# Sigmoid attention and a gated FFN on one core: heads as 64 partitions of seven tokens, QK and PV in array quarters, PV first in five bursts a batch

## The chip, the core and the metric

The kernel runs on one core of one Trainium2 chip. The metric is the device time of one execution in microseconds (us). Most executions of one kernel agree within 0.3%. The kernel before took 435.05 us in the median of the three runs (433.63 to 435.94).

## The reference

Eight batches, twelve heads, 448 tokens, head size 64; then an FFN with 768 inputs and 1536 inner units on all 3584 tokens. In float32, cut to its core:

```python
# batch, n_heads, seq, head_dim = 8, 12, 448, 64;  d_model, d_ff = 768, 1536
scores = (1 / sqrt(64)) * q @ k.transpose(0, 1, 3, 2) - log(448)
attn = 1 / (1 + exp(-scores))            # a sigmoid: no sum over the row
x = (attn @ v).transpose(0, 2, 1, 3).reshape(3584, 768)
gate = maximum(x @ w_gate, 0)
out = (gate * (x @ w_val)) @ w_out       # (3584, 768), float32
```

## The kernel before

The work of the kernel is on TensorE, which writes its results into the banks of a memory called PSUM; another engine then "evicts" a bank, that is, reads it out, before it can be filled again. TensorE does QK (scores transposed, keys in partitions), PV, the two products of the gate and the value ("gv", six matmuls of 448 columns each), and the output product ("down"). ScalarE takes the sigmoids and half of the evictions, VectorE the rest. All of it is programmed in one fixed order. From batch 1 on, attention is cut into bursts, and FFN units of earlier batches stand between the bursts, so that ScalarE has time for the sigmoids.

A batch's 448 tokens do not divide by 128. The kernel before puts them in 128 partitions as three and a half blocks: three blocks of 128 keys and a rest of 64 per pair of heads. Two rests of two pairs share one unit ("R"). A unit is two PSUM banks of scores and one sigmoid for each. QK of a block runs in array halves (64 rows by 128 columns), or in quarters (64 by 64) in bursts that also hold PV. PV has its rest blocks in quarters and its full blocks as 128 rows by 64 columns:

```python
def qk_unit(b, unit, quarters):
    ps = [bank("qk_ps") for _ in range(2)]
    ...                                          # the "R" unit: cut
        pr, c = unit
        qkT = qkT_tiles[(b, pr)]
        for hh in range(2):
            rows = slice(64 * hh, 64 * hh + 64)
            step = 64 if quarters else P
            for o in range(0, P, step):
                nc.tensor.matmul(ps[hh][o : o + step, 0:S],
                    qkT[rows, c * P + o : c * P + o + step], qkT[rows, Q0 : Q0 + S],
                    tile_position=(64 * hh, o), ...)
    PT = PTp.tile([P, 2, S], FP16, tag="PT", name="PT")
    for hh in range(2):
        sigmoid(PT[:, hh, :], ps[hh][:, 0:S])

bursts = [((0, 0), (0, 1), ("R", 0)), ((0, 2), (1, 0), (1, 1)), ((1, 2), (2, 0), (2, 1)),
          ((2, 2), (3, 0), ("R", 1)), ((3, 1), (3, 2), (4, 0)), ((4, 1), (4, 2), ("R", 2)),
          ((5, 0), (5, 1), (5, 2))]
pv_at = {0: (-1, 2), 3: (0, 0), 5: (0, 1)}
...
    for m, burst in enumerate(bursts):
        for unit in burst:
            qk_unit(b, unit, m in pv_at)         # three units, six banks
        if m in pv_at and not (m == 0 and b <= 2):
            ...                                  # PV last: the other two banks
        ...                                      # transposes of later pairs by DMA
            ffn_mix(mix[m])
```

The banks come from a pool of eight, handed out in turn; an allocation waits until the last reader of that bank is done. Batch 0 is laid out differently: 112 partitions of four tokens, two halves of 224 queries, transposed on TensorE. Batch 1 is transposed on TensorE too, and from batch 2 on VectorE copies keys and queries together ("rel") and a DMA transposes them ("qkT").

## Time and profile before

| | before |
|---|---|
| time, median of 3 runs | 435.05 us |
| span of the profiled execution | 432.6 us |
| TensorE busy | 423.6 us, 98% |
| DMA-transposed pairs (36), median from issue to landing | 4.0 us |
| first sigmoid starts at | 7.22 us |

The span can be cut where the gv work on batch 1 and on batch 2 begins, since both kernels pass these points with nearly the same work done (the changed kernel is four QK units, 0.76 us, ahead at the first point and one, 0.19 us, at the second). This is the view of three stretches of the kernel before. Its columns are the stretch, its length, the busy time and number of instructions of TensorE, of its weight loads, of VectorE, ScalarE and GpSimd, then the granted clock, the DMA share and GB/s.

```profile
0.00:67.53 67.53, 63.39 (x744) 45.99 (x744) 31.57 (x91) 47.62 (x88) 37.92 (x60) 1.00 1.32 184
67.53:118.32 50.79, 50.23 (x339) 24.78 (x337) 19.90 (x55) 27.79 (x62) 20.27 (x34) 1.00 1.01 134
118.32:432.60 314.28, 309.99 (x1994) 160.16 (x1992) 100.06 (x241) 138.96 (x304) 44.94 (x72) 1.00 0.50 78
```

The reader is to see the full clock in all three stretches, and a TensorE that is idle for some 4 us in each of the first and the last stretch.

### The profile page before, as it was taken

The numbers are of one execution on the slowest core, as the hardware profiler recorded it, in microseconds if no ns is written. First come the engines' busy times: TensorE is split into PE (matmuls) and PEld (weight loads), VectorE is DVE, ScalarE is ACT, GpSimd is POOL, SyncE is SP. The second block draws the span as 40 slices with busy tenths as digits, with TensorE's granted clock in tenths as the row PEclk, the third lists the DMA queues.
The fourth block names the chain that finished last, engine by engine and source line by source line (L and its number), as shares of the span: only waits on it lengthen the run. The fifth ranks groups of instructions, "written<-read, shape, count | busy, mean of one in ns | idle before, by whom it ended". The sixth has DMA issues, their size and how long they took to land.

```text
span 432.6 us, 7728 instructions
## 1 busy us (share of the span) xinstructions
PE 423.6 (98%) x3071; PEld 230.9 (53%) x3071; DVE 151.5 (35%) x385; ACT 214.4 (50%) x452; POOL 103.1 (24%) x165
## 2 busy tenths in 40 slices
PE   8899999999999999999999999999999999999996
PEld 3579765454555455455455555455454554555563
DVE  2473644334242333334242332433233322222111
ACT  5774783566544554645454453654635446122110
POOL 8454816273070201720053200710000000000000
PEclk9999999999999999999999999999999999999999
DMA  9999999699298821996169550992212411100134
GB/s 185 197 196 196 131 202 167 80 146 234 65 145 106 123 59 40 158 116 97 21 95 179 87 91 17 135 131 66 58 44 49 83 23 36 38 0 2 49 98 109
DMA packets 91940, 43.83 MB, mean 101 GB/s; under 512 B 58432, under 2 KB 88320, under 8 KB 91904
## 3 DMA queue, kind: packets, MB, share of 16 engines
q0 software_dynamic: 52896, 23.14, 44.0%
q1 hardware_dynamic: 38448, 19.67, 23.8%
q10 hardware_dynamic: 560, 0.52, 0.4%
q8 instruction: 24, 0.39, 0.4%
q14 instruction: 12, 0.10, 0.1%
HBM read 47.19 MB, written 11.01 MB: 135 GB/s over the span
## 4 chain that ended last, share of the span: by engine, by line
PE 91%; DMA 4%; ACT 2%; DVE 1%; issue 0%; ACTq 0%
PE g_ps L358 26%; PE v_ps L358 24%; PE ya L412 16%; PE yb L412 8%; PE qk_ps L306 6%; PE pv_ps L341 6%; DMA qkT<-rel 4%; ACT PT L191 2%; PE qk_ps L220 1%; PE pv_ps L327 1%; PE pv_ps L238 1%; PE warm_ps L174 1%; PE qk_ps L290 1%; DVE qkT L207 1%; PE trt L277 1%; DVE xT L182 0%
## 5 line engine op out<-in xcount | busy, mean ns | idle before, releaser
L191 ACT ACTIVATE PT<-qk_ps 128x448 f16<-128x448 f32 (+1 forms) x318 | 154.0, 589 | 26.1 <-PE qk_ps L306 21.4
L358 PE MATMUL g_ps<-xT,wg 128*128 128x448 f16 (+1 forms) x648 | 127.7, 333 | 0.2 <-DVE xT L182 0.2
L358 PE MATMUL v_ps<-xT,wv 128*128 128x448 f16 (+1 forms) x648 | 126.8, 332 | 0.0
L376 DVE TENSOR_TENSOR hT<-gate_sb,v_ps 128x448 f16<-128x448 f32 (+1 forms) x108 | 61.2, 569 | 161.4 <-PE v_ps L358 91.7
L367 ACT ACTIVATE gate_sb<-g_ps 128x448 f32<-128x448 f32 (+1 forms) x102 | 53.4, 531 | 78.9 <-PE g_ps L358 78.7
L412 PEld LDWEIGHTS <-hT 128*128 128x128 f16 x672 | 65.7, 98 | 47.2 <-issue 0.4
L358 PEld LDWEIGHTS <-wg 128*128 128x128 f16 x648 | 58.5, 98 | 57.2 <-issue 19.1
L358 PEld LDWEIGHTS <-wv 128*128 128x128 f16 x648 | 63.2, 98 | 46.4 <-issue 0.4
L412 PE MATMUL ya<-wo,hT 128*128 128x512 f16 x336 | 77.1, 379 | 0.0
L426 ACT ACTIVATE ysb<-yb 128x256 f32<-128x256 f32 x28 | 10.7, 384 | 105.2 <-PE yb L412 105.2
L182 DVE TENSOR_SCALAR xT<-pv_ps 128x448 f16<-128x448 f32 (+1 forms) x54 | 29.7, 573 | 46.5 <-PE pv_ps L341 41.1
L412 PE MATMUL yb<-wo,hT 128*128 128x256 f16 x336 | 41.3, 273 | 0.0
L420 DVE TENSOR_SCALAR ysb<-ya 128x512 f32<-128x512 f32 x28 | 19.4, 692 | 56.7 <-PE ya L412 56.7
L306 PE MATMUL qk_ps<-qkT 64*64 64x448 f16 (+1 forms) x336 | 33.0, 357 | 0.1
L112 POOL DMA_DIRECT2D v<-in_v_dram x13 | 9.1, 699 | 94.6 <-PE pv_ps L341 66.4
L341 PE MATMUL pv_ps<-PT,v 128*64 128x448 f16 x252 | 27.8, 357 | 0.0
L106 POOL DMA_DIRECT2D k<-in_k_dram x15 | 10.3, 686 | 35.4 <-DVE rel L260 32.2
L341 PEld LDWEIGHTS <-v 128*64 128x64 f16 x252 | 12.5, 109 | 11.3 <-issue 5.0
L306 PEld LDWEIGHTS <-qkT 64*64 64x64 f16 (+1 forms) x336 | 9.1, 99 | 16.5 <-issue 13.3
L119 POOL DMA_DIRECT2D v<-in_v_dram x21 | 13.3, 635 | 16.9 <-DMA q<-in_q_dram 12.0
L118 POOL DMA_DIRECT2D v<-in_v_dram x21 | 13.5, 641 | 8.9 <-DMA wo<-in_moe_w_out_dram 6.4
L117 POOL DMA_DIRECT2D v<-in_v_dram x21 | 14.0, 665 | 0.0
(44 smaller groups left out, 171.4 us busy)
## 6 DMA issues: line engine op xcount, KB each, us to landing
out_dram<-ysb SPq DMA_DIRECT2D x48, 192.0 KB, 2.7
wg<-in_moe_w_gate_dram POOLq DMA_DIRECT2D x6, 384.0 KB, 10.2
wv<-in_moe_w_val_dram POOLq DMA_DIRECT2D x6, 384.0 KB, 10.6
wo<-in_moe_w_out_dram POOLq DMA_DIRECT2D x1, 1536.0 KB, 11.9
k<-in_k_dram POOLq DMA_DIRECT2D x6, 256.0 KB, 5.2
q<-in_q_dram POOLq DMA_DIRECT2D x6, 256.0 KB, 6.9
v<-in_v_dram POOLq DMA_DIRECT2D x21, 64.0 KB, 7.4
k<-in_k_dram POOLq DMA_DIRECT2D x9, 128.0 KB, 5.5
```

Source lines behind the costliest of these rows:

```text
L117: nc.gpsimd.dma_start(v16[64:P, odd, :], hi[:, o, :])
L118: nc.gpsimd.dma_start(v16[64:P, even, 0:KLO], hi[:, e, 0:KLO])
L119: nc.gpsimd.dma_start(v16[0:64, even, KLO:], hi[:, e, KLO:])
L182: nc.vector.tensor_scalar(out=xT_of(b, pr)[:, q0 : q0 + qn], in0=src, scalar1=XSCALE, scalar2=None, op0=AOP.mult,)
L191: nc.scalar.activation(PT_ap, ps_ap, AF.Sigmoid, bias=sig_bias, scale=qk_scale)
L306: nc.tensor.matmul(ps[hh][o : o + step, 0:S], qkT[rows, c * P + o : c * P + o + step], qkT[rows, Q0 : Q0 + S], start=True, stop=True, tile ...
L341: nc.tensor.matmul(ps[r][64 * hh : 64 * hh + 64, 0:S], v16[:, 2 * pr + hh, c * D : (c + 1) * D], PT[:, hh, :], start=False, stop=(c == 2), ...
L358: nc.tensor.matmul(ps[-1][:, 0:qn], wt[:, dc, f * P : (f + 1) * P], xT_tiles[(b, dc)][:, q0 : q0 + qn], start=(dc == 0), stop=(dc == NDC - 1),
L367: nc.scalar.activation(gate_sb[:, 0:qn], ps[0][:, 0:qn], AF.Relu)
L376: nc.vector.tensor_tensor(out=hT_tiles[(g, f)][:, o : o + qn], in0=gate_sb[:, 0:qn], in1=ps[1][:, 0:qn], op=AOP.mult,)
L412: nc.tensor.matmul(ps[:, 0 : m1 - m0], hT_tiles[(g, f)][:, t * P : (t + 1) * P], wo[:, f, m0:m1], start=(f == 0), stop=(f == NFC - 1),)
L420: nc.vector.tensor_scalar(out=ysb[:, m0:m1], in0=ps[:], scalar1=OUT_SCALE, scalar2=None, op0=AOP.mult)
```

## The change

Every batch is laid out as 64 partitions of seven tokens per head, with two pairs of heads side by side in 128 partitions (a "group" of four heads; three groups a batch). All of QK and PV can then run in array quarters. The intent is plain from the kernel before: one tiling mode for a whole burst, five bursts instead of seven, hence fewer changes of mode, and no rest blocks. PV stands first in its burst. Batch 0 is cut into 192 and 256 queries, and has six slots of four units instead of twelve of two. The core of the diff, cut at "...":

```diff
-    CH = 112
-    NCH = S // CH
+    NCH = S // 64
+    QCUT = 3
+    HALVES = ((0, QCUT), (QCUT, NCH))
...
+    def load(b, g0, g1, which="kqv", c0=0):
+        for nm, t16, src in zip("kqv", tiles_of(b), (k, q, v)):
+            if nm in which:
+                for g in range(g0, g1):
+                    for r in range(2):
+                        nc.gpsimd.dma_start(
+                            t16[64 * r : 64 * r + 64, g, :, c0 * D :],
+                            rows_of(src, b, r)[:, g, :, c0 * D :],
+                        )
...
+    def qk(qkT, r, hh, c, c0, c1, out_ap):
+        rows = slice(64 * hh, 64 * hh + 64)
+        cols = slice(64 * r, 64 * r + 64)
+        nc.tensor.matmul(out_ap, qkT[rows, c, cols], qkT[rows, NCH + c0 : NCH + c1, cols],
+            tile_position=(64 * hh, 64 * r), ...)
+
+    def pv(b, g, q0, qn, pieces):
+        ps = [bank("pv_ps") for _ in range(2)]
+        for c in range(NCH):
+            for hh in range(2):
+                for r in range(2):
+                    rows = slice(64 * r, 64 * r + 64)
+                    nc.tensor.matmul(ps[r][64 * hh : 64 * hh + 64, 0:qn],
+                        v16[rows, g, hh, c * D : (c + 1) * D], pieces[c][rows, hh, :],
+                        start=(c == 0), stop=(c == NCH - 1),
+                        tile_position=(64 * r, 64 * hh), ...)
+        for r in range(2):
+            put_xT(b, 2 * g + r, q0, qn, ps[r][:, 0:qn])
...
+        cuts = (0, 4, 7, 11, 16, 21) if b <= 2 else (0, 4, 8, 12, 16, 21)
+        pv_at = {0: -1, 3: 0, 4: 1} if b <= 2 else {0: -1, 2: 0, 4: 1}
...
+        for m in range(5):
+            if m in pv_at and (b, m) != (1, 0):
+                ...                              # PV first
+            for g, c in order[cuts[m] : cuts[m + 1]]:
+                qk_unit(b, g, c)                 # four or five units
+            if b == 1:
+                if m == 0:
+                    load(2, 0, 1, "kq")
+                    load_o()                     # the output weights, 2.3 MB
+                    load(2, 1, 2, "kq")
+                    ...
+                if m == 3:
+                    dma_transposes(2, 0)
```

Batch 2 begins with the PV of batch 1 and QK of its own first group. Its first group is transposed by a DMA during batch 1.

## The prediction

> **What bounds the kernel now.** I read the page first: its list of engines, then the chain of work that ended last, then the waits of TensorE.
>
> ```profile
> PE 423.6 (98%) x3071; PEld 230.9 (53%) x3071; DVE 151.5 (35%) x385; ACT 214.4 (50%) x452; POOL 103.1 (24%) x165
> ...
> PE 91%; DMA 4%; ACT 2%; DVE 1%; issue 0%; ACTq 0%
> ```
>
> ```profile
> PE qk_ps L220 <- DVE qkT L207: 1.8, 3, 0.7
> PE warm_ps L174 <- DVE zeros L137: 1.2, 1, 1.2
> PE qk_ps L220 <- ACT PT L191: 0.4, 1, 0.4
> PE qk_ps L290 <- DMA qkT<-rel: 0.4, 1, 0.4
> PE g_ps L358 <- DVE xT L182: 0.2, 1, 0.2
> ```
>
> The reader is to see that TensorE carries 91% of the chain, and that its listed waits add up to 4.0 us of 432.6. From batch 2 on it waits for nobody. So what counts is matmul time, what stands between matmuls, and any new wait. The next view is the timeline of TensorE in a steady stretch (start, length, engine, line, op; an entry's length includes the matmul's pipeline tail, so I take differences of starts):
>
> ```profile
> 194.67 0.35 PE L358 MATMUL v_ps<-xT,wv 128*128 128x448 f16 x1
> 194.95 0.74 PE L306 MATMUL qk_ps<-qkT 64*128 64x448 f16 x6
> 195.63 1.31 PE L358 MATMUL g_ps<-xT,wg 128*128 128x448 f16 x6
> 196.77 1.30 PE L358 MATMUL v_ps<-xT,wv 128*128 128x448 f16 x6
> ...
> 200.50 1.47 PE L412 MATMUL yb<-wo,hT 128*128 128x256 f16 x12
> 201.90 0.57 PE L306 MATMUL qk_ps<-qkT 64*64 64x448 f16 x8
> 202.31 0.36 PE L290 MATMUL qk_ps<-qkT 64*64 64x448 f16 x4
> 202.49 0.36 PE L327 MATMUL pv_ps<-PT,v 64*64 64x448 f16 x4
> 202.78 1.33 PE L341 MATMUL pv_ps<-PT,v 128*64 128x448 f16 x12
> 204.04 1.31 PE L358 MATMUL g_ps<-xT,wg 128*128 128x448 f16 x6
> ```
>
> Six full matmuls of 448 columns take 1.14 us, 0.19 each. Four quarters together also take 0.19 (202.31 to 202.49), and so does a pair of halves. I call 0.19 a slot. A burst without PV runs from 194.67 to 195.63, 0.96 us, in which are the last full matmul and three slots, 0.76: 0.20 are lost at its two borders. A burst with PV starts when the last of twelve yb matmuls of 0.109 does, at 201.70, and ends at 204.04: 2.34 less 0.11 and ten slots of 0.19 leaves 0.33, for three borders (202.49 to 202.78 is 0.29 where 0.19 would do). With the slightly longer first full matmuls after it I count 0.21 and 0.35.
>
> **What the Trainium skill says.** "TensorEngine Tiling (Array Packing)", Key Properties: changing the tiling mode, not just the tile, drains TensorE. The trace agrees: about 0.1 us per border, and none between QK and PV quarters. "TensorE: Matmul & The Clock Gate", Back-to-back issue gap: N/2.4 + 2.5 ns, 189 ns for 448 columns; the trace has 190. Same page, Part 3, What overlaps and what doesn't: matmuls keep strict order, so one that waits holds all behind it; the waits above do not contradict it. "PSUM — Partial Sum Buffer", Specifications: 8 banks per partition, a matmul output at most one. No run shows the number 8, but the program names eight banks, and the kernel before fits them exactly: three QK units of two banks plus PV's two.
>
> **The change part by part.**
>
> *Matmul work, batches 1 to 7: nothing.* 147 QK units and 21 PV groups of 7 slots stay 147 slots each. TensorE gets 3660 matmuls instead of 3071, since quarters go four to a slot; that costs nothing here, as four quarters took the 0.19 of two halves.
>
> *Borders: a saving.* Before: 49 bursts, 19 of them with PV, and two PV groups alone: 30 x 0.21 + 21 x 0.35 = 13.7 us. After: 35 bursts and one PV alone, all in quarters: 36 x 0.21 = 7.6. Saved **6.1 us**. The transposes of batch 1 become column halves with their own borders, 3 x 0.2 = 0.6 back.
>
> *PSUM banks: a new wait.* A burst now has four or five QK units, so 8 or 10 banks, and with PV 10 or 12. In order: PV takes two, units 0, 1 and 2 the other six, and unit 3 needs a bank that PV just filled. I let the changed kernel's instructions be listed with their banks and waits: of 20 PV bursts, unit 3 gets both PV banks in 10; in the other 10 it gets one PV bank and the first bank of unit 0, and the second PV bank goes to what comes next. When are they free? These are the timelines of VectorE and ScalarE:
>
> ```profile
> 195.13 0.62 DVE L376 TENSOR_TENSOR hT<-gate_sb,v_ps 128x448 f16<-128x448 f32 x1 [1.65 <-PE v_ps L358]
> ...
> 203.58 1.19 DVE L182 TENSOR_SCALAR xT<-pv_ps 128x448 f16<-128x448 f32 x2 [2.19 <-PE pv_ps L341]
> ```
>
> ```profile
> 195.35 2.73 ACT L191 ACTIVATE PT<-qk_ps 128x448 f16<-128x448 f32 x6 [0.88 <-PE qk_ps L306]
> ```
>
> The first pair's last PV slot starts at 202.78 + 0.21 + 0.19 = 203.18, its eviction 0.40 later; two evictions take 1.19. In the new PV both banks fill in the same last slot; call its start s. The evictions end at s + 1.02 and s + 1.59, and a semaphore adds some 0.04. TensorE would reach unit 3 at s + 4 x 0.19 = s + 0.76. Where it needs both banks it loses 1.63 - 0.76 = 0.87 us. In the other case: unit 0 starts at s + 0.19, its sigmoid 0.40 later, and lasts about 0.54 (six take 2.73, overlapped), so unit 3 goes at s + 1.17, a loss of 0.41, and the unit or FFN matmul after it loses 0.15 to 0.25 on the second PV bank: 0.6. Sum: 10 x 0.87 + 10 x 0.6 = **14.7 us**.
>
> *The same in bursts without PV.* Of these, 13 have a fourth unit that takes the bank of the FFN unit just before. Its eviction starts 0.46 after the last matmul (194.67 to 195.13) and takes 0.62, free at 1.12; TensorE arrives at 0.28 + 0.20 + 0.19 + 0.19 = 0.86. 13 x 0.26 = **3.4 us**.
>
> Both lie wholly on TensorE, which has no slack to absorb them.
>
> *Batch 0: about even.* Here ScalarE sets the pace: 24 sigmoids of 2 x 448 at 0.85 us, 20.4 us. From 0.455 for 448 columns and 0.85 for 896 I estimate 0.88 ns a column plus 0.06: 0.74 for 768, 0.96 for 1024. The new three slots of 192 and three of 256 queries then take 3 x (3 x 0.74 + 0.40) + 3 x (3 x 0.96 + 0.51) = 18.0. TensorE saves 1.1 us: 96 slots of 0.096 become 42 of 0.083 or 0.109. Against it: between the units now stand about a dozen pieces of 0.6 to 1.2 us (14 transpose pairs, a PV, an FFN unit), two score buffers let TensorE run only two units ahead, and only 4 FFN units of 192 queries fill this stage instead of 6 of 224. I estimate 0.2 to 0.5 us of ScalarE waiting at most of them, about what is gained: 0, give or take 2. Some 1 us of ScalarE-made gaps in batch 1 (53.04 to 54.16 in the timeline) may go too.
>
> *Transfers: hidden.* Input pieces grow from 384 or 512 bytes to 896 in the tile, which can only help; the relay copies halve in number; the tail is unchanged.
>
> Sum: -6.1 + 0.6 + 14.7 + 3.4 + 0 - 1 = +11.6 us on 435.05.
>
> **The rivals.** *First, the borders win:* bank waits are small because PV goes first and three units cover its eviction. Then only -6.1 + 0.6 - 1 counts, 428 to 430. Against it: three slots are 0.57 us, and two evictions plus their start 1.59. For it: whoever ordered PV first meant this. *Second, batch 0 decides:* queries of 192 let FFN start after three slots instead of six; a stage without ScalarE gaps would give 2 to 3 us, one with more of them, or inputs landing late behind more than a dozen small loads of 0.7 us issue each, would cost as much. *Third, quarters cost more than a slot* because QK's queries are now read in runs of 64 instead of one run of 448: 0.02 us on 147 slots would be 3 us more. The old bursts have four quarters in 0.19, but never such reads. *Fourth, a transfer blocks VectorE:* the copies for batch 2 stand in batch 1's fourth burst, about when its keys land behind the weights (estimate from 193 KB per us: near 50 us); a delay of 3 us there would still hide behind free banks.
>
> **Range and chances.** The mechanism is firm, its size rests on four measured durations and a count of bursts. If the bank waits are a third smaller, +5.6; if batch 0 also loses 2 us and quarters cost more, +16. I predict **446 us**, range 437 to 454. Slower by 2% means over 443.8: chance 0.64. Within 2%: 0.30. Faster by 2% (under 426.3) would need no waits and a better batch 0: 0.06.
>
> **What would show it.** In the new profile TensorE's waits must list QK behind VectorE's eviction of PV, about 20 times, up to 0.9 us, together with about 13 behind the FFN's product and 10 behind sigmoids, 15 to 20 us in all; border gaps must still be 0.1, five pairs a batch; four quarters must start 0.19 apart. Batches 2 to 7 should take some 10 us longer together. If there are no such waits, or if the time before batch 1's first QK changes by more than 3 us, I was wrong in that step.

## More of the kernel before

Some executions differ by the clock granted to TensorE (1.00 is full), of which the text tells where it matters.

Batch 2 begins with the PV of batch 1 and five FFN units ahead of its first QK.

## The result, and the profile after

The changed kernel took **451.80 us** in the median of four runs (449.25 to 454.94), beside 434.76 us (433.63 to 435.94, four runs) for the kernel before. The ratio is 1.0395, with a 95% interval of 1.031 to 1.048: slower. A ratio here is the mean time of one kernel's runs over that of the other's in the same rounds, so it is not quite the ratio of the medians that I quote. The four executions fall into two kinds: two with a mean granted clock of 0.98 took 453.81 and 454.94, two with 0.999 took 449.25 and 449.79. The profiled one is of the slower kind.

From the page of the changed kernel: engines, clock in 40 slices, and the chain of work that ended last.

```profile
PE 434.1 (96%) x3660; PEld 241.8 (53%) x3660; DVE 129.6 (29%) x247; ACT 211.9 (47%) x453; POOL 97.7 (22%) x163
...
PEclk8599998999999999999999999999999999999999
...
PE 87%; DMA 5%; DVE 3%; ACT 3%; issue 1%; ACTq 0%
```

Against the page of before, TensorE gave up four points of the chain, and VectorE, ScalarE and DMA took them. The clock row has two dents: slices 1 and 2, and slice 7. The kernel before had none. The waits of TensorE after:

```profile
PE qk_ps L215 <- DVE xT L167: 4.8, 29, 0.2
PE qk_ps L215 <- DMA qkT<-rel: 2.4, 1, 2.4
PE trt L190 <- ACT k L380: 2.4, 1, 2.4
...
PE trt L190 <- DVE q L381: 0.9, 1, 0.9
```

The first line is the predicted wait, QK behind the eviction of PV. The second is a wait on the DMA transposes of batch 2's first group, and the third and fourth are waits for the first keys and queries. The stretches after, cut at the same points:

```profile
0.00:76.54 76.54, 66.99 (x989) 48.41 (x989) 27.49 (x67) 46.44 (x92) 41.01 (x68) 0.91 1.23 176
76.54:129.10 52.56, 51.62 (x388) 26.35 (x385) 15.23 (x30) 26.43 (x60) 21.97 (x38) 0.97 1.03 138
129.10:453.10 324.00, 315.46 (x2291) 167.03 (x2288) 86.88 (x152) 139.02 (x305) 34.72 (x59) 1.00 0.40 71
```

So the profiled execution lost 9.0 us up to the FFN of batch 1, 1.8 us in the second stretch and 9.7 us in the last, which runs at full clock. The last stretch is what I had predicted to lose. The first one I had called about even.

**The bank waits.** Here is a burst with PV, and one without, in TensorE's timeline of the changed kernel:

```profile
92.74 1.23 PE L215 MATMUL qk_ps<-qkT 64*64 64x448 f16 x16
93.91 1.31 PE L293 MATMUL g_ps<-xT,wg 128*128 128x448 f16 x6
...
102.45 1.52 PE L232 MATMUL pv_ps<-PT,v 64*64 64x448 f16 x28
103.80 0.74 PE L215 MATMUL qk_ps<-qkT 64*64 64x448 f16 x12
104.69 0.35 PE L215 MATMUL qk_ps<-qkT 64*64 64x448 f16 x1 [0.15 <-DVE xT L167]
105.22 0.57 PE L215 MATMUL qk_ps<-qkT 64*64 64x448 f16 x7 [0.18 <-DVE xT L167]
```

And VectorE's timeline at that time:

```profile
104.01 1.16 DVE L167 TENSOR_SCALAR xT<-pv_ps 128x448 f16<-128x448 f32 x2 [2.07 <-PE pv_ps L232]
```

PV's last slot begins at 103.80 less 0.19, that is 103.61; three units of four quarters follow at 103.80; the fourth would start at 103.80 + 3 x 0.19 = 104.37. It has its first matmul at 104.69 and its second at 105.22, when the second of VectorE's two evictions is done (104.01 + 1.16 = 105.17). The delay is 0.85 us, though the wait that the view prints is only 0.15 + 0.18. The printed idle begins where the previous matmul's modelled end lies, 0.35 us after its start, so short waits look far smaller than they are. Only differences of starts tell the loss. This is why the sum of 4.8 us in the list of waits explains only part of the 9.7 us.

I therefore computed for each burst from batch 3 on: the start of the first FFN matmul behind it, less the start of the last one before it, less 0.19 for each slot of four quarters or two halves and the time of that last FFN matmul. This is the mean loss per burst in us (with its count; a burst is named by its number of QK units):

| | before | after |
|---|---|---|
| QK alone, three units | 0.20 (20) | |
| QK alone, four units | | 0.50 (10) |
| three units and PV | 0.36 (14) | |
| four units and PV | | 0.78 (5), 1.10 (5) |
| five units and PV | | 1.06 (5) |

**The transfer.** The same timeline where batch 2 begins:

```profile
71.26 1.52 PE L232 MATMUL pv_ps<-PT,v 64*64 64x448 f16 x28
75.20 1.40 PE L215 MATMUL qk_ps<-qkT 64*64 64x448 f16 x16 [2.42 <-DMA qkT<-rel]
76.53 2.24 PE L293 MATMUL g_ps<-xT,wg 128*128 128x448 f16 x6
78.57 2.09 PE L293 MATMUL v_ps<-xT,wv 128*128 128x448 f16 x6
80.50 1.30 PE L293 MATMUL g_ps<-xT,wg 128*128 128x448 f16 x6
```

The DMA transposes were issued at 59.71 and TensorE got their result at 75.20. Besides the wait itself, six matmuls of 448 columns now take 2.04 us (76.53 to 78.57) instead of 1.14: TensorE was put to half clock, and stayed there until about 80.2.

### The profile page after: what moved, and what is told of

The parts are those of the page before. It is cut to its first block, busy times and chain, and to the rows that moved or that the text cites.

```text
span 453.1 us, 8742 instructions
## 1 busy us (share of the span) xinstructions
PE 434.1 (96%) x3660; PEld 241.8 (53%) x3660; DVE 129.6 (29%) x247; ACT 211.9 (47%) x453; POOL 97.7 (22%) x163
## 3 DMA queue, kind: packets, MB, share of 16 engines
q0 software_dynamic: 32960, 23.28, 36.8%
## 4 chain that ended last, share of the span: by engine, by line
PE 87%; DMA 5%; DVE 3%; ACT 3%; issue 1%; ACTq 0%
PE g_ps L293 24%; PE v_ps L293 23%; PE ya L331 16%; PE yb L331 8%; PE qk_ps L215 7%; PE pv_ps L232 7%; DMA qkT<-rel 3%; DVE xT L167 3%; ACT PT L176 3%; PE trt L190 2%; DMA ysb<-in_q_dram 1%; DVE qkT L195 0%; ACTq L110 0%; PE warm_ps L159 0%; ACT ysb L345 0%
## 5 line engine op out<-in xcount | busy, mean ns | idle before, releaser
L176 ACT ACTIVATE PT<-qk_ps 128x448 f16<-128x448 f32 (+3 forms) x318 | 150.8, 596 | 65.2 <-PE qk_ps L215 65.1
L293 PE MATMUL g_ps<-xT,wg 128*128 128x448 f16 (+2 forms) x648 | 128.5, 334 | 0.8 <-DVE xT L167 0.2
L293 PE MATMUL v_ps<-xT,wv 128*128 128x448 f16 (+2 forms) x648 | 127.6, 333 | 0.0
L311 DVE TENSOR_TENSOR hT<-gate_sb,v_ps 128x448 f16<-128x448 f32 (+2 forms) x108 | 60.9, 569 | 229.0 <-PE v_ps L293 118.5
L302 ACT ACTIVATE gate_sb<-g_ps 128x448 f32<-128x448 f32 (+2 forms) x104 | 55.3, 549 | 73.1 <-PE g_ps L293 71.3
L215 PE MATMUL qk_ps<-qkT 64*64 64x448 f16 (+2 forms) x756 | 56.2, 347 | 9.1 <-DVE xT L167 4.8
L215 PEld LDWEIGHTS <-qkT 64*64 64x64 f16 x756 | 25.3, 110 | 38.2 <-issue 25.9
L232 PE MATMUL pv_ps<-PT,v 64*64 64x448 f16 (+2 forms) x756 | 38.1, 338 | 0.1
L167 DVE TENSOR_SCALAR xT<-pv_ps 128x448 f16<-128x448 f32 (+2 forms) x54 | 28.4, 568 | 23.2 <-PE pv_ps L232 23.2
L97 POOL DMA_DIRECT2D q<-in_q_dram x48 | 28.8, 622 | 18.7 <-DMA wo<-in_moe_w_out_dram 15.8
```

The source lines that it names most:

```text
L97: nc.gpsimd.dma_start(t16[64 * r : 64 * r + 64, g, :, c0 * D :], rows_of(src, b, r)[:, g, :, c0 * D :],)
L167: nc.vector.tensor_scalar(out=xT_of(b, pr)[:, q0 : q0 + qn], in0=src, scalar1=XSCALE, scalar2=None, op0=AOP.mult,)
L176: nc.scalar.activation(PT_ap, ps_ap, AF.Sigmoid, bias=sig_bias, scale=qk_scale)
L215: nc.tensor.matmul(out_ap, qkT[rows, c, cols], qkT[rows, NCH + c0 : NCH + c1, cols], start=True, stop=True, tile_position=(64 * hh, 64 * r ...
L232: nc.tensor.matmul(ps[r][64 * hh : 64 * hh + 64, 0:qn], v16[rows, g, hh, c * D : (c + 1) * D], pieces[c][rows, hh, :], start=(c == 0), sto ...
L293: nc.tensor.matmul(ps[-1][:, 0:qn], wt[:, dc, f * P : (f + 1) * P], xT_tiles[(b, dc)][:, q0 : q0 + qn], start=(dc == 0), stop=(dc == NDC - 1),
```

## The experiments

Twelve kernels ran, all with correct results. My theory at first was that banks explain the last stretch, and that batch 0 with its late first loads explains the first one. The rivals were that the order PV first is harmless and something else in the quarters costs the time, and that the first stretch is lost to the transfer. Each result below stands beside 433.6 to 434.5 us for the kernel before in the same rounds.

**Seven bursts of three units, PV still first.** No burst needs more than eight banks then.

```diff
-        cuts = (0, 4, 7, 11, 16, 21) if b <= 2 else (0, 4, 8, 12, 16, 21)
-        pv_at = {0: -1, 3: 0, 4: 1} if b <= 2 else {0: -1, 2: 0, 4: 1}
+        cuts = (0, 3, 6, 9, 12, 15, 18, 21)
+        pv_at = {0: -1, 3: 0, 5: 1}         # and the FFN units shared out over seven
```

> The changed kernel with seven bursts of three QK units a batch instead of five of four or five; PV still first and all in quarters, so PV and three units fill exactly eight banks. Bank theory: the waits for PV's eviction (0.6 to 0.9 us in each of 20 bursts) and for the FFN product go, some 15 to 17 us, and 14 more bursts cost 14 x 0.21 = 2.9 us: 436 to 440 us against 451.8. Rival (quarters, strided query reads or batch 0 cost the time, not banks): 452 to 456 us.

Measured: 442.38 us (439.27 to 445.85), ratio 1.0192 (1.0124 to 1.0259). The waits of TensorE in this run:

```profile
PE qk_ps L215 <- DMA qkT<-rel: 3.4, 1, 3.4
PE g_ps L293 <- DVE xT L167: 3.1, 20, 0.2
```

QK no longer waits for the eviction of PV. But now the FFN product behind each of the 20 PV bursts gets PV's bank, and waits in its place: such a burst loses 0.44 us, where borders alone cost 0.22. The bank theory holds in kind; the time came out 2.4 us above my range because I had not asked who gets the bank next, and because the wait on the transfer grew from 2.4 to 3.4 us. The clock plays a part too: the two executions at 0.994 and 0.997 took 439.27 and 440.57 us, the two at 0.979 took 444.19 and 445.85.

**PV two units behind in its burst, nothing else.**

```diff
-            if m in pv_at and (b, m) != (1, 0):
-                ...                              # PV
-            for g, c in order[cuts[m] : cuts[m + 1]]:
+            ahead = 2
+            for n, (g, c) in enumerate(order[cuts[m] : cuts[m + 1]]):
+                if n == ahead and m in pv_at and (b, m) != (1, 0):
+                    ...                          # PV
                 qk_unit(b, g, c)
```

> The changed kernel with the same instructions and the same five bursts, only PV moved behind two QK units of its burst instead of before them all. Bank theory: PV's banks are then asked for again only in the fifth unit or the FFN after the burst, where they come from a unit whose sigmoids are done, so the PV waits shrink from about 0.7 to under 0.2 us a burst: 437 to 441 us. The waits of 0.26 us in bursts without PV stay. Rival (the burst's length or the quarters as such cost the time): 450 to 453 us, as no instruction is added or taken away.

Measured: 442.57 us (440.85 to 443.92), ratio 1.0192 (1.0158 to 1.0225). A burst of five units and PV in its timeline:

```profile
110.82 0.57 PE L215 MATMUL qk_ps<-qkT 64*64 64x448 f16 x8
111.22 1.49 PE L232 MATMUL pv_ps<-PT,v 64*64 64x448 f16 x28
112.54 0.98 PE L215 MATMUL qk_ps<-qkT 64*64 64x448 f16 x12
113.46 1.31 PE L293 MATMUL g_ps<-xT,wg 128*128 128x448 f16 x6
```

No wait of QK on an eviction of PV is left in the list. Four units with PV lose 0.22 us now, which is the two borders, and five lose 0.47. From batch 2's FFN to the end the profiled run took 314.8 us, against 324.0 with PV first and 314.3 before. So 9.2 of the 9.7 us of the last stretch are the order of PV and the banks. The quarters themselves cost no more than a slot: eight of the new kind, with their queries in runs of 64, take 0.40 us (110.82 to 111.22), two slots of 0.19 and 0.02.

**PV three units behind (a dose).**

```diff
-            ahead = 2
+            ahead = 3
```

> A dose test of the bank theory: the changed kernel with PV behind three QK units of its burst instead of two. Bank theory: with two units ahead TensorE waited for no PV eviction (442.6 us). With three ahead, PV takes the banks of the last FFN product, whose eviction is not over, so each of the 20 PV bursts waits about 0.26 us again, as the bursts without PV do: 447 to 448 us with a wait of PV on the FFN product in the list, and no QK wait on the eviction of PV. Rival (what counts is only that PV is not first in its burst): the same as with two ahead, 442 to 443 us.

Measured: 447.86 us (444.10 to 449.27), ratio 1.0308 (1.0252 to 1.0364). The same place in its timeline:

```profile
109.81 0.76 PE L215 MATMUL qk_ps<-qkT 64*64 64x448 f16 x12
110.40 1.77 PE L232 MATMUL pv_ps<-PT,v 64*64 64x448 f16 x28
111.83 0.72 PE L215 MATMUL qk_ps<-qkT 64*64 64x448 f16 x8
```

PV's 28 matmuls stretch from 1.32 to 1.43 us by their starts. The starts of single matmuls in this trace show why: the first one is at 110.40, the second, which writes the other bank, only at 110.66. VectorE's eviction of the FFN product (hT) had ended at 110.60. By my sum over starts, a burst of four units with PV loses 0.50 us instead of 0.22 and one of five 0.59 instead of 0.47. The list of waits does not print this wait, since the first matmul's modelled end covers it, so that part of the expectation missed. That the time was right is luck in part: two of the four runs had clocks of 0.974 and 0.977, and the two at 0.99 took 444.10 and 446.57 us. In the stretch from batch 2's FFN to the end, 318.7 us against 314.8 and both at full clock, the dose costs 3.9 us. It is the bank that counts, not the mere place of PV.

**The first loads.** The second group's loads, which share the DMA engines with the first group's, are held until the first keys are there.

```diff
-    load(0, 1, 2, "kq")
     ident = const.tile([P, P], FP16, name="ident")
     make_identity(nc, ident[:])
+    hold = const.tile([P, 2], FP32, name="hold")
+    nc.gpsimd.tensor_copy(hold[0:1, :], k32[1][0:1, 0:2])
+    load(0, 1, 2, "kq")
```

> The changed kernel with GpSimd's loads of the second group held back until the first key rows have landed. Theory: the first head group landed late (8.5 us against 6.4) because these loads now start 2 us earlier on the same engines and share them; then the first sigmoid moves from 10.55 to 7.5 to 8.5 us and the time falls by 2 to 3.5 us, 448 to 450 us. Rival (loads of 64 partitions land late by themselves): first sigmoid stays at 10 us or later, time 451 to 454.

Measured: 451.41 us (450.86 to 454.31), ratio 1.0411 (1.0372 to 1.0451): no gain. The first sigmoid did start at 7.44 instead of 10.55 us. Its waits:

```profile
PE trt L192 <- DMA q<-in_q_dram: 2.7, 2, 1.5
PE qk_ps L217 <- DMA qkT<-rel: 1.9, 1, 1.9
```

The second group is late in its turn, and the first FFN unit started only 1.1 us earlier (23.28 for 24.34). That the loads as a whole pace the early stage would fit this, but is not shown: the granted clock differs too, half from 12.7 to 16.1 and from 19.5 to 22.9 us here, from 8.5 to 22.1 us in the changed kernel. Behind the wait of 1.9 us the clock stayed full.

**Batch 2's first group transposed on TensorE instead of by DMA.**

```diff
-                if m == 3:
-                    dma_transposes(2, 0)
+            hooks = {..., 4: [(1, lambda: both(2, 0))]}    # 28 transposes on TensorE
```

> The changed kernel with the first group of batch 2 transposed on TensorE (two times 28 quarter-width transposes, about 1.1 us) instead of by a DMA that landed 15 us after its issue. Theory: the gap of 2.4 us before batch 2's first QK goes, and with it the half clock after it (1.7 us in the profiled run): 447 to 450 us and a mean granted clock of 0.99 or more. Rival (the gap moves to the next transfer, group 1 of batch 2): TensorE waits for qkT at the next burst by about as much, time 450 to 453.

Measured: 450.30 us (448.98 to 452.32), ratio 1.0362 (1.0332 to 1.0392). The wait on the transfer and the second dent in the clock are gone, and the profiled run reached batch 1's FFN at 75.02 instead of 76.54 us, batch 2's FFN at 125.58 instead of 129.10. The second number is the one to read, since the half clock came behind the first point. Both profiled runs had half clock at the start, and the whole span fell by 3.0 us (450.1 for 453.1), as much as the wait and the half clock less the transposes seemed to be worth (2.4 + 1.7 - 1.0). The medians fell by 1.5 us only. Two executions of each kernel had a clock of 0.999, and there the transposes on TensorE gained nothing: 450.09 and 450.51 us against 449.25 and 449.79. No such execution was profiled.

**Bursts of five and three.** PV two behind, the transposes on TensorE, and from batch 3 on no burst without PV that has a fourth unit.

```diff
-        cuts = ... else (0, 4, 8, 12, 16, 21)
+        cuts = ... else (0, 5, 8, 13, 16, 21)
```

> PV two units behind, batch 2's first group transposed on TensorE, and from batch 3 on bursts of 5, 3, 5, 3 and 5 units, so that no burst without PV has a fourth unit. Bank theory: 442.6 less 1.5 (the transposes, as measured alone) less 10 x 0.27 (the fourth units) = 438 to 439 us; from batch 2's FFN to the end about 312 us against 314.8 with two ahead alone and 314.3 before. Rival (fourth units lose nothing that counts; fifth units lose more): 441 us, about 315 us.

Measured: 435.70 us (435.44 to 437.64), ratio 1.0051 (1.0020 to 1.0082). This is 3 us better than I expected, but not for my reason. The last stretch took 314.0 us, not 312: QK alone lost 0.22 us per burst as hoped, but every PV burst now had five units and lost 0.47. The gain was up to batch 1's FFN (72.15 for 75.40 us with PV two behind alone). With PV two behind, the transfer's wait had been 4.4 us; taking it away was worth more than in the run before, where it had been 2.4.

**Batch 0 as the kernel before has it**, whole, with its 112 partitions, its loads and its schedule; once on top of the last kernel, and once as the only thing undone.

```diff
-        self.g, (self.c0, self.c1) = g, HALVES[half]     # 64 x 7 tokens, 192 and 256 queries
+        self.pr, self.q0 = pr, q0                        # 112 x 4 tokens, 224 and 224 queries
...                                                       # with load_first, first_transposes, the loop
```

> The kernel of the run above, with batch 0 as the kernel before has it whole: 112 partitions of four tokens, halves of 224 queries, its loads, its schedule; batches 1 to 7 in quarters. Theory (what is left of the loss lies in the new batch 0 and its loads): first sigmoid near 7.2 us, the first FFN of batch 1 near 69 instead of 75 us, 431 to 433 us in all, below the kernel before. Rival (the loss before batch 1's FFN comes from the quarter layout of batch 1, or from the weights and inputs landing as before): 436 us or more.

Measured: 434.61 us (434.30 to 435.83), ratio 1.0021 (0.9995 to 1.0048): as fast as the kernel before, no faster, and 1.1 us faster than with the new batch 0, less than the 3 to 5 us that I had expected. The first FFN of batch 1 came at 69.35 us as expected; the remaining 1.8 us against the kernel before are four QK units of batch 2 moved forward, 0.76 us, and 1.0 us of transposes that a DMA did in the kernel before.

> The changed kernel with nothing undone but batch 0, which is as the kernel before has it whole. Theory (batch 0 carries 5 to 7 of the 17 us): 444 to 447 us, the first FFN of batch 1 near 70 us instead of 76.5, and from batch 2's FFN to the end still about 324 us. Rival (batch 0 is even, as I predicted): 450 to 452 us.

Measured: 451.52 us (449.53 to 452.32), ratio 1.0392 (1.0353 to 1.0432): no gain over the changed kernel in the medians. My theory of the first stretch, which asked for 444 to 447 us, fell here. This is its timeline:

```profile
66.60 1.52 PE L244 MATMUL pv_ps<-PT,v 64*64 64x448 f16 x28
71.77 1.71 PE L227 MATMUL qk_ps<-qkT 64*64 64x448 f16 x16 [3.65 <-DMA qkT<-rel]
73.41 2.42 PE L337 MATMUL g_ps<-xT,wg 128*128 128x448 f16 x6
```

With the old batch 0, TensorE comes to this point 4.7 us earlier (PV at 66.60 for 71.26), and waits 3.65 us for the transfer instead of 2.42, again with half clock behind it. The transposes were issued 3.3 us earlier (56.43 for 59.71) and again took 15 us. So 1.2 of the 4.7 us were spent on waiting, and the whole span of this profiled execution is 3.1 us shorter (450.0 for 453.1). The medians are even because two executions of the changed kernel, at a clock of 0.999, took 449.25 and 449.79 us, no more than the one at 0.998 here (449.53). They were not profiled; that the late transfer hides the slow start there would fit, but is not shown.

**The transfer held apart from the weights.** The same kernel, and GpSimd issues the output weights and the rest of batch 2 only when the transposes have landed.

```diff
                 if m == 3:
                     dma_transposes(2, 0)
+                    nc.gpsimd.tensor_copy(gate[0:1, :], qkT_tiles[(2, 0)][0:1, 0, 0:2])
+                    load(2, 1, 2, "kq")
+                    load_o()
+                    ...                          # the rest of batch 2, moved here from m == 0
```

> The changed kernel with batch 0 as before (451.5 us when run alone), and one thing more: GpSimd starts the loads of the output weights and of the rest of batch 2 only when the DMA transposes of batch 2's first group have landed. Transfer theory (the transposes were not hidden because they shared the DMA engines with 2.3 MB of output weights issued just before them): they land 5 to 7 us after their issue instead of 17, TensorE's wait of 3.7 us on them and the stretch of half clock after it go, the first FFN of batch 1 starts near 68.5 instead of 73.4 us, and the time is 446 to 447 us. Rival (the transposes are slow in themselves, or the wait is paid later when the held loads land late): 450 to 452 us.

Measured: 450.49 us (450.34 to 451.49, five runs), ratio 1.0377 (1.0360 to 1.0393). The time is the rival's; the mechanism is the theory's. These two lines of its profile are the issue of the transposes, on SyncE, and the first instruction of GpSimd that waits for them:

```profile
56.48 15.87 SPq L220 DMA_TRANSPOSE qkT<-rel  x2
61.00 0.17 POOL L504 COPY gate<-qkT 1x2 f16<-1x2 f16 x1 [11.97 <-DMA qkT<-rel]
```

They took 4.5 us (56.48 to 61.00) instead of 15.3 (56.43 to 71.77 in the run before). So the loads issued ahead of them were what made them late; the weights and the other loads of batch 2 were held together, and which of the two counts is not set apart. The first group was in time, with no wait, and batch 1's FFN started at 69.73 instead of 73.41 us. Then the held loads came late. TensorE and VectorE of this run, 15 us on:

```profile
84.25 0.56 PE L227 MATMUL qk_ps<-qkT 64*64 64x448 f16 x5
87.27 1.65 PE L227 MATMUL qk_ps<-qkT 64*64 64x448 f16 x11 [2.46 <-DVE hT L355]
```

```profile
76.82 0.62 DVE L355 TENSOR_TENSOR hT<-gate_sb,v_ps 128x448 f16<-128x448 f32 x1 [1.65 <-PE v_ps L337]
85.23 0.39 DVE L216 COPY rel<-k 128x896 f16<-128x896 f16 x1 [7.79 <-DMA k<-in_k_dram]
```

VectorE stood for 7.79 us before the copy of keys that had not landed. The FFN products behind it in its queue stayed in their banks, and QK waited for those banks. Most of the gain was lost again 15 us later, by another way (batch 2's FFN began at 124.62 instead of 125.89 us): a late transfer blocked VectorE, which was my fourth rival, only not where I had put it.

**The transposes on TensorE, with the old batch 0.** This takes the transfer away without making another one late.

```diff
+        # batch 0 as before, whole
-                if m == 3:
-                    dma_transposes(2, 0)
+            hooks = {..., 4: [(1, lambda: both(2, 0))]}
```

> The changed kernel with batch 0 as before and with batch 2's first group transposed on TensorE, its loads as in the changed kernel: nothing is held, so nothing lands later. In the run with batch 0 alone the wait on the DMA transposes was 3.7 us and the half clock after it cost about 1.7; the transposes on TensorE cost about 1.0. Theory (the transfer's wait and its half clock are real time): 451.5 - 5.4 + 1.0 = 447 us, the first FFN of batch 1 near 70 us; what is left against the kernel before, some 12.5 us, is then the bank waits less the borders. Rival (the wait only moves again): 450 to 451 us.

Measured: 446.72 us (446.39 to 447.25, five runs, all with a clock of 1.000), ratio 1.0291 (1.0271 to 1.0310), as the theory had it to 0.3 us. Its stretches:

```profile
0.00:70.20 70.20, 65.08 (x889) 48.20 (x890) 28.79 (x72) 48.05 (x91) 39.66 (x64) 1.00 1.29 191
70.20:121.06 50.86, 49.92 (x384) 25.85 (x384) 15.74 (x31) 26.31 (x59) 19.26 (x34) 1.00 1.02 137
121.06:444.70 323.64, 315.45 (x2291) 167.12 (x2288) 86.89 (x152) 139.02 (x305) 34.71 (x59) 1.00 0.41 71
```

The clock is full throughout. Of the 12.1 us that this profile is longer than that of the kernel before, 9.4 are in the last stretch and 2.7 in the first, of which 1.8 are the four QK units and the transposes named above. So taking the transfer away gained 451.5 - 446.7 = 4.8 us with the old batch 0. The transposes on TensorE took some 1.0 us of that back, so I estimate the late transfer itself at 5.8 us, and what remains of 446.7 - 434.1 = 12.6 us for the bursts at 11.6.

**A version that uses what was learned.** From batch 2 on six bursts of 4, 3, 4, 3, 4, 3 units, PV two behind in those of four, the transposes on TensorE; once with the old and once with the new batch 0.

```diff
+        cuts = (0, 4, 7, 11, 16, 21) if b == 1 else (0, 4, 7, 11, 14, 18, 21)
+        pv_at = {3: 0, 4: 1} if b == 1 else {0: -1, 2: 0, 4: 1}
```

> Batch 0 as before, batches from 2 on in six bursts of 4, 3, 4, 3, 4, 3 units, PV two units behind in those of four. From the losses measured per burst (0.22 us for three units alone and for four with PV two behind, 0.50 for four alone, 0.47 for five with PV): a batch loses 6 x 0.23 = 1.4 us instead of 1.9, so about 2.7 us less than the 434.6 of the same kernel in bursts of five and three: 431.5 to 432.5 us, 0.4 to 0.6% below the kernel before. Rival (each burst's borders cost the same whatever its units): 435 us or more.

Measured: **431.28 us** (431.04 to 432.46, six runs), ratio 0.9931 (0.9917 to 0.9945): 0.7% faster than the kernel before, with an interval clear of 1. A burst with PV, and the last stretch:

```profile
131.51 0.57 PE L227 MATMUL qk_ps<-qkT 64*64 64x448 f16 x8
131.92 1.49 PE L244 MATMUL pv_ps<-PT,v 64*64 64x448 f16 x28
133.24 0.55 PE L227 MATMUL qk_ps<-qkT 64*64 64x448 f16 x8
133.72 1.31 PE L337 MATMUL g_ps<-xT,wg 128*128 128x448 f16 x6
```

```profile
117.63:428.90 311.27, 307.17 (x2292) 162.12 (x2288) 88.12 (x155) 138.62 (x304) 35.94 (x60) 1.00 0.41 74
```

From batch 2 on every burst with QK loses 0.22 us now, with PV or without, and the last stretch is 3.0 us shorter than before. This is what the quarters save here.

> The same six bursts with the new batch 0 (the changed kernel's layout throughout, batch 2's first group transposed on TensorE). Theory: 2.7 us less than the 435.7 of the same kernel in bursts of five and three, 432.5 to 434 us; and 0 to 2 us slower than the run with batch 0 as before, which is then what the new batch 0 costs. Rival (batch 0 costs 5 us or more): 437 us or more.

Measured: 433.65 us (432.09 to 434.58, six runs), ratio 0.9978 (0.9957 to 0.9999). It falls into two kinds again: 432.09, 432.42 and 432.91 us at clocks of 0.998 and 0.999, and 434.39, 434.50 and 434.58 at 0.982 and 0.983. The profiled execution is of the second kind:

```profile
8.00:12.00 4.00, 3.73 (x52) 2.15 (x52) 1.18 (x5) 1.62 (x2) 4.00 (x7) 0.50 1.21 188
12.00:16.00 4.00, 3.58 (x64) 2.26 (x56) 1.43 (x3) 2.78 (x4) 4.00 (x7) 0.50 1.27 174
```

With the old batch 0 no execution is of this kind (0.998 to 1.000 in all six). So the new batch 0 costs about 1.1 us at full clock (mean 432.5 less 431.4) and 3.1 us when half clock is granted in the start, which happened in three of six executions.

## Why the prediction was right or wrong

The prediction named the class (slower, 0.64) and its range held the time; 446.0 stands against 451.8. The mechanism that it named is there, at the size that it named. That the range held although a whole term was missing is owed to the range's width. By its own steps:

- *PSUM banks, +14.7, and bursts without PV, +3.4:* right. Against 0.22 us of borders, a PV burst lost 0.56 or 0.88 us more (I had 0.6 and 0.87), one of five units 0.84, and four units alone 0.28 (I had 0.26). Giving each kind its third of 20 PV bursts, that is 20/15 x (5 x 0.56 + 5 x 0.88 + 5 x 0.84) = 15.2 us, and 13 x 0.28 = 3.6. Taking only PV's place back removed 9.2 of the 9.7 us in the last stretch, and the dose run put 3.9 of them back. The list of waits shows 29 waits on the eviction of PV, but none on the FFN product, for which the prediction had asked about 13 times; they are there in the starts of single matmuls (in the burst at 92.74, the fourth unit's second matmul starts at 93.59 instead of 93.33, behind an eviction that ended at 93.54).
- *Borders, -6.1:* right in size. They cost 0.22 us per burst in quarters, where I had 0.21; the six-burst version shows them as a gain when no wait covers it.
- *The sum of these steps* was +11.6 us. The run that has only them, with the old batch 0 and no transfer to wait for, shows +12.6 (446.72 against 434.09), or 11.6 without its 1.0 us of transposes: it is the kernel that I had in fact predicted. So close a match is luck in part, since the terms as measured, -6.1 + 0.6 + 15.2 + 3.6, add up to 13.3.
- *"Transfers: hidden"* is the step that failed. I had looked at sizes of pieces and number of copies, and not at when batch 2's first keys are needed. In the kernel before, the PV of batch 1 and five FFN units stand ahead of batch 2's first QK; in the new one nothing does, and the DMA transposes share their engines with 2.3 MB of output weights. The term is some +5.8 us instead of 0 (estimate above): a wait of 2.4 us in the changed kernel and 3.7 with the old batch 0, and half clock behind it for 3.4 and 5.6 us. With the loads held back, the same transposes landed after 4.5 us instead of 15.3.
- *"Batch 0: about even", 0 give or take 2:* the medians are even, 451.80 against 451.52 with the old batch 0, but the profiled executions are not, 453.1 against 450.0. In the six-burst kernel it costs 1.1 us at full clock and 3.1 with half clock in the start. I had counted sigmoids (18.0 instead of 20.4 us), and neither the first loads nor the clock.
- *I had said that a change of more than 3 us before batch 1's first QK would mean that I was wrong in that step.* This sign did not show: the first QK came at 38.44 instead of 37.61 us. It was badly chosen, since the changed kernel had by then done only 6.5 us of FFN products instead of 10.3 (in slots of 0.19). The delay came to light later: PV at 71.26 instead of 66.60 us with the old batch 0, and +9.0 us up to batch 1's FFN against the kernel before, the wait on the transfer included.
- *"From batch 2 on it waits for nobody"* misread the kernel before a little: two of its PV bursts lost more than the usual 0.33 us, 1.08 at 103.76 and 0.58 at 187.72.
- *ScalarE's gaps in batch 1, -1:* not settled. No run sets it apart.

In the medians, the old batch 0 alone gained 0.3 us, the transposes on TensorE alone 1.5, and both together 5.1 (446.72); in the profiled executions it is 3.1, 3.0 and 8.4 us. Two delays of which one hides the other would do this, but no execution of the changed kernel with a clock of 0.999 was profiled, so what those wait for stays open.

## What to carry to other kernels

Before putting more work between two stretches of other work, count the PSUM banks in order of allocation, and ask for each bank who read it last and who gets it next; moving one product two units back in its burst was worth 9 us here, the same product three units back lost 4 of them again. When a change pulls the first use of a tile forward, look up when its transfer lands, not how long it takes, and expect that removing one delay uncovers another behind it. A list of waits understates short waits: measure bursts by the starts of matmuls.

## What the Trainium skill lacked or had wrong

- "TensorEngine Tiling (Array Packing)", Key Properties, says that changing the tiling mode drains TensorE, but not what it costs: 0.20 us for a burst of halves with its two borders, 0.22 us for one of quarters, and 0.34 us with three borders, the same to 0.01 us in nearly all of the 34 bursts with QK that were measured in the kernel before.
- "TensorE: Matmul & The Clock Gate", What's actually happening, has half clock come after an idle window of about 3.4 us. Here gaps of 2.4 us (changed kernel, at 75.20) and 2.5 us (loads held, at 87.27) were enough, while one of 1.9 us (first loads, at 73.81) was not. The half clock after the first lasted from 76.8 to 80.2 us, 3.4 us, which agrees with that page's window; at the start of the changed kernel it lasted from 8.5 to 22.1 us, 13.6 us, with TensorE listed as busy for nine tenths of it. Three of six executions of one kernel with this start had the lower clock (0.98), and took 2.0 us longer; what decides it is not shown.
- "DMA: Bandwidth & Descriptors", Issuing engines are not separate DMA queues, says that transfers of all engines interleave on the same 16 DMA engines. DMA transposes that landed 4.5 us after their issue when the loads were held back took about 15 us with 2.3 MB of weights and 0.7 MB of other loads issued in the 8 us before them.
- On no page is how far the printed waits of TensorE fall short: the printed 0.15 + 0.18 us stood for a delay of 0.85 us.
